# Attention and two expert layers on one core: another table for the order and the engine of each operation

## The chip, the core and the metric

The kernel runs on one core of a Trainium2 chip. A core has five engines with queues of their own: TensorE (PE: matrix products, from weights that it loads by PEld), VectorE (DVE), ScalarE (ACT), GpSimd (POOL) and SyncE (SP), which here only issues DMAs. Each engine runs its instructions strictly in the order in which the program gives them; between engines they wait on semaphores. The metric is the device time of one execution in microseconds.

## The reference

```
q_rot, k_rot = rotate(q), rotate(k)                 # 4 batches, 8 heads, 576 tokens, 64 wide
attn = softmax(q_rot @ k_rot.T / sqrt(64)) @ v      # max subtracted before exp
x = attn as 2304 tokens x 512
h = x @ w_in;  g = h * clip(h + 3, 0, 6) / 6;  x = g @ w_out       # layer 1, 512 -> 2048 -> 512
h = x @ w2_in; g = P(h) / (Q(h) + 1e-6);       out = g @ w2_out    # layer 2, same sizes
```

P is a cubic polynomial with coefficients a, and Q = 1 + |b0| |h| + |b1| h^2. All inputs and outputs are float32.

## The kernel before

Each float32 operand is split into a float16 high part and a float16 low part, and a product is made of three float16 products (high by high, high by low, low by high), summed in PSUM. So for each operand there is a cast to the high part, which ACT, DVE or POOL can do (the helper `copy`, whose instruction stands at L313 on ACT, L315 on POOL, L317 or L319 on DVE), and a subtraction that gives the low part.

*Attention* works in units of 128 queries for two heads (1152 score columns), and of 64 left-over queries (640 columns). PE writes the scores s into PSUM (L706 to L717), DVE reduces the maximum mx (L721), a small operation scales it (L724 to L729), ACT makes the exponentials e (L738). Then p is split: high part by `copy`, low part by the subtraction in L760, and a transposing DMA of SP (L763) writes both, turned, into pt, which PE multiplies with v (L796). A few early units use transposes on PE instead. The output xu is normalised (L814 to L826) and turned into xt for layer 1. Queries and keys come as nat, are turned by the rotary angles on DVE (L642, L649) and split.

*Layer 1* runs beside the attention of the following batch: matmuls h of 256 columns (L901), ACT's relu (L908), DVE's clip and product (L910) into t, high part gh by `copy`, low part gl by L914, and the second matmul (L929), which ACT or DVE evicts from PSUM (L935, shown as t<-h,d) and a DMA takes to y1d in DRAM.

*Layer 2* follows when all tokens have passed. It goes by blocks of 512 columns and pairs of feature tiles. A pair's 24 matmuls (L1148) fill a PSUM tile of 1024 columns, hh and hx in turn, one buffer each. The rational function reads it three times on ACT (lq L1157, ls L1158, lt L1159) and twice on DVE (L1163, L1164); after the last of these reads the tile is free for PE. DVE and ACT go on (L1161, L1166 to L1171) to lt, split into lgh (ACT, L1172) and lgl (DVE, L1173), and PE multiplies by w2o into ac (L1183), which goes to the output (ob). The last block has 256 columns. The layer's weights w2i and w2o are scaled and split at its start: the high parts by `copy` (L1050), the low parts by DVE (L1051).

What sets the order: the program makes 3527 operations as objects (`Plan.op`), and `Plan.order` decodes a table, `ORDER` (L93), into a list of pairs, operation and engine letter (P, A, D, G for PE, ACT, DVE, POOL; Q for SP's queue; N for none), with the PSUM bank of the operations that share two banks. The program issues the operations in this list's order, each on its engine, so that the table alone sets each queue.

```
code = np.cumsum(np.frombuffer(zlib.decompress(base64.b85decode("".join(ORDER))), "<u2"), ...) % 65536
for x in code:
    o, e = self.ops[x // 12], "PADGQN"[x % 12 // 2]
```

Of the kernel before, what the change touches and what calls it, by code (L numbers as in the profile page):

```python
# [23 lines left out]
H = 8  # L24
S = 576
D = 64
# [72 lines left out]
    'r)CMfqBr@In8|-Yqeecoz-<A{22c7`zqi`hr9q*<NHbPEwc!^+5=}>W5Y(U38s`S&3O;k1?=p7imT=#9@Q-8AF9h`q&vvxVJoglub9#;^HN0o<',
    'yX)zQ@J09!JerY1w_s5(fzq$1d~x4sbk6WCFddem+mjTTV6$ppAz#!AoAjgT1N7Y3l3y8rB7DPqXz!zPGVi(@4ZF7V>Xf|De%Q-Db`=`Ew8p<0',  # L100
    'tc5^yz%>+Ib1fP{dRJJW1!kvSD~vf)jSZL}wa#M5PpAxyf*9`i_E9lB=P8JG;9}>BUinr0#V*Z&A$?jXMJ{^>*Xt*qe0>0ca0t74fO+JWa2$KW',
    'je)KwIS*p1u@%%rMo}T$(pNpR#sG|KZxT#T;H_Ku3G~q=STK5Mie8zParM#*k!icZyAzs*wS?5GQC*>_LOa^f|19~xMP_92?Gb$;^ci<xpHA}Y',
    '=7H<JG<`K<^avF+1b1N<pTusP<HB87^vEE--GKW-no%me^l4|EbT|3nt;2alYdtepxrs%#3>7zj^3&h-j=en<yhaxk(+)TjE7kJk%!?sfo_s4D',
    'fD}hk49pXu#&{u!j@;NYbMD5lmLJ=I0yyUKVvmdlDL=NymnySDz-WdcF&B!}D)?8zpBhiZRP|KIb+oBxbcJH6BG$(T%{zuex~oo#%ixO58iiW-',
    'S1hs!%SxSa+tI4lNN>sarMB}bq0TW6YszD36<XYF=VekQw7M!ULhdd!Z=QJk7mUX;iHK4SdzVN}(C_S5rnwsWf5=bO;~O7E7va>XbnL5*Qorkt',
    'wyO%B3Oa723SK2we2qW0e_egerwWzulysxNGdQzSUZmM%HI`=*KGU&-(;_>3og>A<!laRBW{7^vAuJoEjzwGx2jOEm$w)C%6O*ki{X)1we&Bra',
    'E<;!ol1Q@puZ5ophjsv)dM=y_JGM*p$w}t1<G_5$cPN6C9?O6Xc~&=-Vd>bsE%X~}h9GsucIlYdt&WQSQ~iVv80Wqk{3<#V+oO++;u~wmpwR~D',
    '#<Wn+R4mQd^X;p;eD7jfNZ@~gFT89K>iGc5jBE*i#(&f7Fi28|@gL1ksp2lul8r4PAba2CIQOJ*B+W3Bn((WuO`6I^X^~_(Lpjm!eC1owzb8d8',
    '!tawoXDR;8*!Q$-xl=C@4(Wh;&#~n`wVU+e*qFFUQW&dujZb2qNDZKnTeJ%`7-js3dL%U%7V)7OAzi89bNNiXqBog}+)K-i5n&Zd@T<@gf6FNY',
    'M5@x^%?7Q6ZCaL|fAK0(Cd*8fM{o38RKb+pg*93MdvugcD|O=ZR}L?7VUuxsh14P~+$eP+6V;GK(#Sox??W%DB|d%DT@Qz$EYC6$(3#yHCGO+U',  # L110
    'fwvYqd=r=7(7xyDrIXl2A83c}A(D!l;8fWZ8|Wf*s~hw{8t|@!!pe^Go_-_}G7mfUkLcI*de<YIYHvrgq+eDqosY3-i^;3+mWUOtca=e3)N<A!',
    'AI-pfb_JAU0c~3AbUK;`-L3*W=?h=Higvr2qj#i5<vZ{RJ)+f8lDbE;q-xvG&C=IO)(1C(=b9kZ!nS>`)k|S=pgP>=TAkFPG=jsuhk^-z_}M2E',
    'yI*Vh?%e1e71`>$^oQ;-6t)`^r#>5(UV1i8o87}~Z%^sC`i9<@hLj8tQcpkIbWP)bQhq2+&>5u|*8OeaS!G$8qx;IbKk4%&Y0;k2mZeF$r<A$_',
    '=rvh@P47r(Nn7_9Up3Hmd<#EGD0){wLf&V=UL58fZvU0ymEp<f_x+VHsij&+q}#g?3i9{dfzKaEBMH@)KAxC${7v_SHXOPq`jN&}LvyG#;Zf*i',
    'LYc&czQ<y7Jzp8>6rZV~R0wT2mdz91PaB{*ROfqs`8;6^2F34&zRnA#z}WfB{Kzp9TTmLMJNz=8ylj+wd?oXg|3LmTnlM=$=TGeba>NFe_QV!i',
# [1174 lines left out]
```

## Time and profile before

| what | us |
|---|---|
| median of 3 runs | 1084.6 |
| fastest and slowest run | 1083.87, 1087.87 |
| the profiled execution | 1082.5 |
| its span (first to last instruction) | 1080.7 |
| PE busy in it | 982.2 |
| DVE, ACT, POOL busy | 905.7, 780.5, 61.2 |

Busy times of different engines lie beside each other and don't add up to the span. An engine's idle time matters only where what it waits for ends last. The span falls into the head (loads, splits of weights and the first units), attention beside layer 1, the end of layer 1, the entry of layer 2 and its body, and a tail. The clock in the rows is the share of full speed that was granted to PE: 1.00 is 2.4 GHz, and a mean of 0.86 over a stretch means that part of it ran at the lower level of 1.2 GHz.

### The profile page before, as it was taken

Reading aid. Unit: us, or ns where it says so; the run is one execution under the profiler, and the core shown is the slowest. Engines: PE = TensorE matmul, PEld = TensorE weight load, DVE = VectorE, ACT = ScalarE, POOL = GpSimd, SP = SyncE. Lnnn points to the kernel's source line nnn. Section 1 sums busy time; section 2 is a strip of 40 time slices with the busy share of each in tenths; the row PEclk is TensorE's granted clock in tenths of the full one; section 3 lists DMA queues with packets and bytes.
Section 4 is the critical chain, followed back from the end, with each engine's and each line's share of the span. In section 5 each row is a group of like instructions: output and inputs, shape, how many; then the busy total and the mean of one; then the engine's idle time right before and its main releaser. Section 6 shows DMA issues by size and latency. Waiting matters only on the chain.

```text
span 1080.7 us, 20026 instructions
## 1 busy us (share of the span) xinstructions
PE 982.2 (91%) x7973; PEld 695.0 (64%) x7978; DVE 905.7 (84%) x1408; ACT 780.5 (72%) x1219; POOL 61.2 (6%) x71
## 2 busy tenths in 40 slices
PE   1388799899999999999999989789999999999996
PEld 1277678788887888788888868234444444444563
DVE  5989998998999989888735695899799787977975
ACT  8989985877777766666738986685776766775763
POOL 0210010110111010120001010000000000000000
PEclk9998899999999999999999999889999999999998
DMA  8968677769889678587737742001011010010010
GB/s 279 265 160 239 120 125 145 170 122 175 145 171 186 139 135 144 102 155 140 133 65 259 229 170 70 10 0 39 1 40 40 1 39 1 20 39 1 1 40 19
DMA packets 253853, 117.04 MB, mean 108 GB/s; under 512 B 223552, under 2 KB 241088, under 8 KB 253760
## 3 DMA queue, kind: packets, MB, share of 16 engines
q1 hardware_dynamic: 253760, 115.77, 47.2%
q8 instruction: 62, 1.02, 0.4%
q14 instruction: 31, 0.25, 0.1%
HBM read 52.83 MB, written 9.44 MB: 58 GB/s over the span
## 4 chain that ended last, share of the span: by engine, by line
PE 63%; DVE 19%; ACT 9%; DMA 4%; issue 3%; POOL 1%; SPq 0%; ACTq 0%; DVEq 0%; POOLq 0%
PE ac L1183 13%; PE h L929 13%; PE h L901 10%; PE hh L1148 8%; PE hx L1148 7%; PE h L796 4%; PE s L706 3%; DVE mx L721 2%; DMA pt<-p 2%; DVE p L760 2%; DVE t L910 1%; DMA raw<-in_moe_w_in_dram 1%; PE h L787 1%; DVE lt L1163 1%; ACT e L738 1%
## 5 line engine op out<-in xcount | busy, mean ns | idle before, releaser
L901 PE MATMUL h<-xt,w 128*128 128x256 f16 x1728 | 199.7, 275 | 11.4 <-ACT xu L313 3.9
L901 PEld LDWEIGHTS <-w 128*128 128x128 f16 x1728 | 169.1, 99 | 33.6 <-issue 12.8
L929 PE MATMUL h<-gh,w 128*128 128x256 f16 x1080 | 190.3, 273 | 0.0
L929 PEld LDWEIGHTS <-w 128*128 128x128 f16 x1620 | 156.5, 98 | 18.8
L1183 PE MATMUL ac<-w2o,lgh 128*128 128x512 f16 x540 | 161.8, 382 | 3.3 <-ACT lgh L1172 3.3
L1148 PEld LDWEIGHTS <-w2i 128*128 128x128 f16 x900 | 89.1, 99 | 108.9 <-issue 24.0
L929 PE MATMUL h<-gl,w 128*128 128x256 f16 x540 | 147.2, 273 | 0.0
L738 ACT ACTIVATE e<-s,mx,qal 128x576 f32<-128x576 f32 (+1 forms) x144 | 114.5, 831 | 7.5 <-POOL mx L729 5.1
L1148 PE MATMUL hh<-x,w2i 128*128 128x512 f16 (+1 forms) x450 | 98.1, 365 | 8.5 <-ACT ls L1158 6.6
L1148 PE MATMUL hx<-x,w2i 128*128 128x512 f16 (+1 forms) x450 | 97.3, 364 | 6.7 <-ACT lq L1157 5.3
L1183 PE MATMUL ac<-w2o,lgl 128*128 128x512 f16 x270 | 102.8, 381 | 0.0
L721 DVE TENSOR_REDUCE mx<-s 128x2 f32<-128x1152 f32 (+1 forms) x80 | 99.1, 1242 | 3.7 <-PE s L709 3.2
L1183 PEld LDWEIGHTS <-lgh 128*128 128x128 f16 x576 | 56.5, 98 | 70.4 <-ACT lgh L1172 3.7
L760 DVE TENSOR_TENSOR p<-e,p 128x1152 f16<-128x1152 f32 (+1 forms) x72 | 89.2, 1239 | 11.3 <-ACT p L313 11.1
L1172 ACT ACTIVATE lgh<-lt 128x1024 f16<-128x1024 f32 (+1 forms) x40 | 38.6, 968 | 66.4 <-DVE lt L1171 43.8
L796 PE MATMUL h<-v,pt 128*128 128x130 f16 (+3 forms) x1440 | 77.4, 209 | 2.7 <-ACT xu L313 1.0
L908 ACT ACTIVATE t<-h,half,d 128x512 f32<-128x512 f32 (+1 forms) x96 | 61.6, 668 | 24.4 <-PE h L901 23.4
L796 PEld LDWEIGHTS <-pt 128*128 128x128 f16 (+1 forms) x1440 | 73.7, 102 | 7.3 <-issue 5.3
L313 ACT ACTIVATE p<-e 128x1152 f16<-128x1152 f32 (+1 forms) x61 | 64.3, 1054 | 12.1 <-DMA pt<-p 10.6
L706 PE MATMUL s<-qkt 64*128 64x512 f16 (+2 forms) x576 | 57.4, 326 | 8.8 <-ACT e L738 6.0
L1169 DVE SCALAR_TENSOR_TENSOR lt<-lt,cg,lr 128x1024 f32<-128x1024 f32 (+1 forms) x40 | 46.3, 1174 | 21.2 <-ACT lr L1167 21.2
L910 DVE SCALAR_TENSOR_TENSOR t<-t,h 128x512 f32<-128x512 f32 x72 | 48.9, 680 | 10.9 <-ACT t L908 10.4
(231 smaller groups left out, 1662.4 us busy)
## 6 DMA issues: line engine op xcount, KB each, us to landing
raw<-in_moe_w_in_dram SPq DMA_DIRECT2D x32, 512.0 KB, 5.1
raw<-in_moe_w_out_dram SPq DMA_DIRECT2D x32, 512.0 KB, 4.4
y1d<-t SPq DMA_DIRECT2D x18, 256.0 KB, 2.8
nat<-in_k_dram SPq DMA_DIRECT2D x16, 256.0 KB, 3.6
nat<-in_q_dram SPq DMA_DIRECT2D x16, 256.0 KB, 3.2
y<-y1d SPq DMA_DIRECT2D x16, 256.0 KB, 4.2
out_dram<-ob SPq DMA_DIRECT2D x16, 256.0 KB, 2.3
vnat<-in_v_dram SPq DMA_DIRECT2D x14, 256.0 KB, 2.9
```

Source lines behind the costliest of these rows:

```text
L313: act.activation(out, in_, AF.Copy, scale=scale)
L706: pe.matmul(s()[:, a:b], lhsT=kq(1, y, 64 * h, 64 * h + 64)[:, cc * 128:cc * 128 + 128], rhs=kq(0, z, 64 * h, 64 * h + 64)[:, c:c + b - a] ...
L721: op("D", c_dve(n), lambda e: vec.reduce_max(mx()[:, 0, 0:g], sv().rearrange("p (g n) -> p g n", g=g), axis=AX.X, negate=True), r=[s], w=[ ...
L738: act.activation(et()[:, h * (n // g):(h + 1) * (n // g)], sv()[:, h * (n // g):(h + 1) * (n // g)], AF.Exp, bias=mx()[:, 1, h:h + 1], sca ...
L760: op(EN("lo"), c_sub(n), lambda e: EL[e].tensor_tensor(ph()[:, n:2 * n], et()[:, 0:n], ph()[:, 0:n], ALU.subtract), r=es + [(ph, 0)], w=[( ...
L796: pe.matmul(ob()[r0:r0 + m, o:o + k], lhsT=w, rhs=vv[:, 0:k], start=(z == 0 and j == 0), stop=(z == 1 and j == 4))
L901: pe.matmul(hp()[:, o:o + NQ], lhsT=wt[kk]()[:, z, c:c + 128], rhs=x, start=(n == 0), stop=(n == 11))
L908: act.activation(seg(t, c, n), seg(hp, c, n), AF.Relu, bias=half(), scale=x()[:, g:g + 1])
L910: op("D", c_dve(2 * NQ), lambda e, t=t, hp=hp: vec.scalar_tensor_tensor(t(), t(), two(-15), hp()[:, 0:2 * NQ], ALU.min, ALU.mult), r=[hp], ...
L929: pe.matmul(yp()[:, o:o + NQ], lhsT=w[:, s_, m_ * 128:(m_ + 1) * 128], rhs=gt()[:, f], start=(f == 0 and z == 0), stop=(f == KF - 1 and z ...
L1148: pe.matmul(hp()[:, x * n:x * n + n], lhsT=wi[kk]()[:, z, c:c + 128], rhs=xt()[:, kk, y, 0:n], start=(i == 0), stop=(i == 11))
L1183: pe.matmul(accs[j][i]()[0:m], lhsT=gt()[:, y * n + x:y * n + x + m], rhs=wt, start=(f == 0 and z == 0), stop=(f == KF - 1 and z == 2))
```

## The change

Only the table is another. It has 64 lines in place of 67, so that every later line of the program has a number lower by 3.

```diff
@@ -91,73 +91,70 @@
 ORDER = (
-    'c-qx@flnMudgoWw(>*iYJ;Q)mc9!QQ1o2ox5FxV!5so015Dsw`=Ou_(gkuSdSmbjMOAvWM4rlo|uf=l2LWuY{mRKB%Sb_*a9A^>YI0SJ##34V9',
...
+    'c-l=_4@?~Cb${Rd+hJyQSz|)?Hk?BUb&-o4WD$bgjfE(6C`B%^h>Iw4iG>hy=><9NX>&p@@*$UV2tqD(s6|{vsYP6JMJ}?aODQ=aN-fUfEJ7TM',
...
 )
```

The 3527 operations and what they compute are the same. On PE the same 7859 instructions follow in nearly the same order (neighbours are swapped; the farthest move is 9 places). DVE has 1376 instructions in place of 1408, ACT 1053 activations in place of 1105, POOL 151 in place of 67. SP gives 20 DMA issues to ACT: 3 of raw weights, 6 of y1, 2 of y1d, 6 of queries, 3 of values.

Operations that change their engine, over the whole program: from DVE to POOL 16 subtractions L760 (13 of 1152 columns, 3 of 640), 18 subtractions L914 (12 of them between 210 and 560 us of the trace of before, 6 after), 13 operations of the rotary stage, 3 casts of p, 4 of xu, 3 maxima, 2 of gh, 3 casts of layer-2 weights. From ACT to POOL 8 casts gh, 8 maxima, 6 casts of p, 5 in the rotary stage, 10 casts of weights, and two others. From ACT to DVE 11 maxima, 6 casts of p, 8 evictions of xu, 3 casts gh, 6 of weights, and four others. From DVE to ACT 4 casts of p, 3 evictions of layer 1 and 2 maxima. From POOL to ACT 4 of v and 2 maxima, to DVE 3 each of gh, maxima and xu.

Three places follow. The first is ACT's queue where layer 1 ends and layer 2 begins (h_75 and h_76 are the two PSUM banks of layer 1, w2qs a scale, x_9240 the split input of a later block). Before:

```order
L313 ACTIVATE t<-h_75,d 128x2x64 x4
L313 ACTIVATE w2i_9170<-w2o_8364,w2qs 128x512
L313 ACTIVATE w2o_9185<-w2o_8407,w2qs 128x512
L313 ACTIVATE w2o_9200<-w2o_8484,w2qs 128x512
L313 ACTIVATE w2o_9209<-w2o_8466,w2qs 128x512
L313 ACTIVATE w2o_9212<-w2o_8521,w2qs 128x512
L1159 ACTIVATE lt<-hh,cg 128x1024
L1069 ACTIVATE x_9240<-y_8781 128x512 x4
L1157 ACTIVATE lq<-hh,cf 128x1024
L313 ACTIVATE w2o_9250<-w2o_8591,w2qs 128x512
L1158 ACTIVATE ls<-hh,dv 128x1024
```

After:

```order
L310 ACTIVATE t<-h_75,d 128x2x64 x4
L441 ACTIVATE junk,w2am<-w2o_8953 128x512
L310 ACTIVATE t<-h_76,d 128x2x64 x4
L938 DMA y1d<-t 128x2x256
L1156 ACTIVATE lt<-hh,cg 128x1024
L1155 ACTIVATE ls<-hh,dv 128x1024
L310 ACTIVATE w2o_9256<-w2o_8596,w2qs 128x512
L1154 ACTIVATE lq<-hh,cf 128x1024
```

Before, five casts of weights (one of w2i, four of w2o) stand between the eviction t and the first read of hh, and four casts of x and one of w2o among its reads. After, both evictions are ACT's, no cast stands ahead of the first read, and one stands among the reads.

The second is ACT's queue in the last block of layer 2, which has 512 columns in each tile. Before:

```order
L1159 ACTIVATE lt<-hh,cg 128x512
L1159 ACTIVATE lt<-hx,cg 128x512
L1157 ACTIVATE lq<-hh,cf 128x512
L1157 ACTIVATE lq<-hx,cf 128x512
L1158 ACTIVATE ls<-hh,dv 128x512
L1158 ACTIVATE ls<-hx,dv 128x512
L1166 ACTIVATE lr<-lq,qb 128x512 x2
L1167 ACTIVATE lr<-lr 128x512 x2
L1172 ACTIVATE lgh<-lt 128x512 x2
```

After:

```order
L1156 ACTIVATE lt<-hh,cg 128x512
L1169 ACTIVATE lgh<-lt 128x512
L1155 ACTIVATE ls<-hh,dv 128x512
L1169 ACTIVATE lgh<-lt 128x512
L1154 ACTIVATE lq<-hh,cf 128x512
L1156 ACTIVATE lt<-hx,cg 128x512
L1154 ACTIVATE lq<-hx,cf 128x512
L1155 ACTIVATE ls<-hx,dv 128x512
L1163 ACTIVATE lr<-lq,qb 128x512
L1164 ACTIVATE lr<-lr 128x512
```

Before, each step of hx follows the same step of hh. After, the reads of hh stand first, among them the last step (lgh) of the pair ahead, and those of hx behind them.

The third is POOL's queue in the middle of attention, beside layer 1 (the numbers behind p, xu and v are buffers). Before:

```order
L315 TENSOR_SCALAR xu_714<-xu_714 128x256
L315 TENSOR_SCALAR gh<-t 128x512 x3
L315 TENSOR_SCALAR v_111<-vnat_97,qps 128x10x64
L729 TENSOR_SCALAR mx<-mx,qal 128x2
L315 TENSOR_SCALAR xu_714<-xu_714 128x256
```

After:

```order
L757 TENSOR_TENSOR p_2980<-e,p_2980 128x1152
L312 TENSOR_SCALAR xu_742<-xu_742 128x256
L757 TENSOR_TENSOR p_3154<-e,p_3154 128x1152
L757 TENSOR_TENSOR p_3157<-e,p_3157 128x1152
L312 TENSOR_SCALAR xu_592<-xu_592 128x256
L312 TENSOR_SCALAR p_3301<-e 128x1152
L911 TENSOR_TENSOR gl<-t,gh 128x512
```

Before, POOL has only operations with one input tile. After, subtractions of two tiles, p and gl, stand among its casts.

## Rows read from the trace of the kernel before

**Rows 1.** the page: busy time, share of the span and instructions of each engine

```profile
PE 982.2 (91%) x7973; PEld 695.0 (64%) x7978; DVE 905.7 (84%) x1408; ACT 780.5 (72%) x1219; POOL 61.2 (6%) x71
```

**Rows 2.** windows: length; PE, PEld, DVE, ACT, POOL busy; clock; DMA; GB/s

```profile
0.00:150.00 150.00, 93.98 (x707) 80.31 (x708) 133.06 (x267) 135.22 (x282) 12.72 (x17) 0.95 0.79 206
150.00:560.00 410.00, 399.18 (x4516) 343.12 (x4515) 362.60 (x580) 285.85 (x457) 39.22 (x45) 1.00 0.76 141
560.00:676.00 116.00, 109.74 (x941) 92.69 (x941) 73.77 (x152) 90.68 (x181) 9.24 (x9) 0.99 0.54 178
676.00:726.00 50.00, 37.32 (x146) 15.42 (x147) 43.34 (x47) 37.65 (x42) 0.00 (x0) 0.86 0.02 6
726.00:1040.00 314.00, 310.51 (x1492) 145.92 (x1493) 270.88 (x333) 210.53 (x227) 0.00 (x0) 1.00 0.06 19
```

**Rows 3.** timeline of PE, 686 to 726 us: start, duration, instruction, [idle before <-releaser]

```profile
686.40 8.16 PE L1148 MATMUL hh<-x,w2i 128*128 128x512 f16 x24 [4.65 <-ACT ls L1158]
...
702.20 5.34 PE L1148 MATMUL hh<-x,w2i 128*128 128x512 f16 x24 [1.85 <-ACT lq L1157]
...
718.07 7.70 PE L1148 MATMUL hx<-x,w2i 128*128 128x512 f16 x24 [5.35 <-ACT lq L1157]
```

**Rows 4.** timeline of ACT and DVE, 673 to 685 us

```profile
673.38 0.72 ACT L313 ACTIVATE w2o<-w2o,w2qs 128x512 f16<-128x512 f32 x1 [0.82 <-DVE w2i L1051]
674.14 0.75 DVE L1051 SCALAR_TENSOR_TENSOR w2o<-w2o,w2qs,w2o 128x512 f16<-128x512 f32 x1 [0.79 <-ACT w2o L313]
675.22 1.13 DVE L319 TENSOR_SCALAR t<-h,d 128x128 f32<-128x128 f32 x4 [0.33 <-PE h L929]
...
679.21 1.19 ACT L1159 ACTIVATE lt<-hh,cg 128x1024 f32<-128x1024 f32 x1
...
682.32 1.27 DVE L1164 SCALAR_TENSOR_TENSOR lt<-lt,cg,hh 128x1024 f32<-128x1024 f32 x1
683.62 1.11 ACT L1157 ACTIVATE lq<-hh,cf 128x1024 f32<-128x1024 f32 x1 [1.15 <-DVE lt L1164]
```

**Rows 5.** chain that ended last, from 1050 us: start, duration, piece

```profile
1054.15 2.63 PE hh L1148 x24
...
1067.80 6.95 PE ac L1183 x24
```

**Rows 6.** waits: who <- releaser: us in all, number, longest

```profile
PE ac L1183 <- ACT lgh L1172: 3.3, 1, 3.3
PE h L901 <- DVE t L910: 3.3, 3, 2.5
```

**Rows 7.** groups by line and shape: xcount | busy us, mean ns | idle before

```profile
L760 DVE TENSOR_TENSOR p<-e,p 128x1152 f16<-128x1152 f32 x56 | 75.7, 1351 | 9.6 <-ACT p L313 9.5
L914 DVE TENSOR_TENSOR gl<-t,gh 128x512 f16<-128x512 f32 x72 | 49.2, 684 | 6.2 <-ACT gh L313 3.0 <-POOL gh L315 3.0
L319 DVE TENSOR_SCALAR w2i<-w2i,w2ps 128x512 f16<-128x512 f32 x10 | 4.8, 483 | 0.1
L908 ACT ACTIVATE t<-h,half,d 128x128 f32<-128x128 f32 x32 | 12.0, 456 | 3.2 <-PE h L901 2.7 <-DVE gu L1101 0.4
```

**Rows 8.** timelines of POOL and DVE around 140 and 231 us

```profile
140.75 0.62 POOL L315 TENSOR_SCALAR gh<-t 128x512 f16<-128x512 f32 x1 [3.53 <-DVE t L910]
140.64 1.36 DVE L721 TENSOR_REDUCE mx<-s 128x2 f32<-128x1152 f32 x1
...
230.69 1.48 DVE L649 TENSOR_TENSOR nat<-nat,tab 128x1280 f32<-128x1280 f32 x1
230.84 1.80 POOL L315 TENSOR_SCALAR gh<-t 128x512 f16<-128x512 f32 x1 [11.75 <-DVE t L910]
232.68 0.69 DVE L914 TENSOR_TENSOR gl<-t,gh 128x512 f16<-128x512 f32 x1 [0.52 <-POOL gh L315]
```

**Rows 9.** SP's queue: an issue in the timeline, and waits of the transposing DMA

```profile
18.11 0.53 SPq L412 DMA_DIRECT2D raw<-in_moe_w_in_dram  x1
...
SPq L763 <- DVE p L760: 31.8, 18, 4.4
```

More of the change, by code (lines that the diff above doesn't have):

```diff
@@ L99 @@
[L99 to L103, printed above, removed]
@@ new lines @@
+    'fh8!l^Xak@b*5NITou|-T9^sWc^H=K@SKZQG1*{u<<WGz&;^sq11P2?utWlI)moHe1e}Nxfjf-*rqJGiPTGPRm~tyo?fd>9w8H5AdEXj6O+KQ(',
+    'ug3N_r46^wi$b|ljwfF6ne499BTu6@Hf)n^`*AP31Xf~)4k}R?vr81y?o-Cm8xgoF*CoOMll?>DT_p&8%DF@!P-f3rGtkafpwlneH_?7c2p5E4',
+    '>*En9m19mhwEDa7=_7kX?y&<9S6bm~>?1n@FW5sii_z>Y$p18|biue?YVS&Jx=U>I$8yI$9>SC6ab2sTCTe|+zg7F`T0z^#At>_);O1U$FbLI%',
+    'gEi=2M%u`+tTq@`3Sf#U_7I#AXT(x_+S+2mo5R~}h`}b9qrGIUK>M`Lo6Ir5*zXQpurGNdqyv4qjuC7}`={7i!M%@z>Qw&F>q#~YA$h<WRa;r3',
+    ')b2+1*XVTa2|K3z3HvK@&)Slo!F`zbM_JSBFnpN*FZ<(&fl-tcv`;CWL<0(=u&S?q;u_U@)9Y0^l)JDsrA}v>Xar8PtG+ullsmD18_%snuh%QX',
@@ new lines @@
+    '_B48opIfcWTaAcF12v2I>%o9)iT3zU1Ft1F)9W97?cgaB)+p}UVxR<IQ!2~6lvFt3R{2+6H)E{aFKn?++Qw$~H~nLYCMb}cOaW#>cZz4B$-3D^',
+    'qk{c==7)AMN*~nJ)W%oi>y|WQHppk>+RU=FV8)bAX%?o<evHzXeio*jMrqP%m+!$tb4nkg`I&aPBWHw22cw7~lbtn#5XoPCU2FWp+e=mG2E-jH',
+    ';J!9MQWWR1F~T;I<?uMCN1r_~%-_|1o8%FTR&O^4!)VVj5>K4a0x+7>V3&Ad0rNBYT#Lf6V@qEq0rQ1cmfDb`%5!g-1VJ?m)djCndYOtF;pAx}',
+    '03Rd+@S&_jqtCJoc*Fu|vj!#NW2;!Ym1%MUFeT^tF!FGeenn{~H>?W5vOZ86?B{lw-+)|OhdFyk3nAiTPN_TsSHVe+=~3srG4YuO0cBGXlw*6l',
+    '+FKbezX@N<QmI;)bd9GwXOvaDOS!HL*bj_vCv{|y09>$_gAY=}cG1yA`-7~XKbF2_-aOj3({8lVUD<X11N`u=qr(U*(u&-;cxEpE53=#R=yQ_+',
@@ new lines @@
+    'qs+X`>I`eA=;(E;HB$xe$$qGIt^~H&#{OUAeCeRtMwBUF1V2-c29XIPN-r6pPnboIxtlbk<Yxwz0oo__yRV!L<pDC|AdNYVzIW13eG9Pa^^%Ds',
+    '_sBOu$GjRzv`NEiE1g58zQpdMKMQiZys2cn!Pg+a;j0O1y^)jw=9lt7i_NP|cyA>y`npu8VMAW8&?*eO<)#6}vY@W#ZSL%1cI6{Z&m9CI>Rj^&',
+    '@OhP4;V-2zan#$$E84A0<Uy5xMCd?Nj<NcKliFQ~dHE!tRHRDvSLRnyx9yy1l+l}7_JzfmIjq((SL`-ZzFc_I(vkh@pk6gd6a=gwv+kDg+?!$x',
+    '>Err1TcuAAHs7GXY|ELT=i#(ac%(L7ZAR4~jHC@H(>GiVR?^MtHrq|VVD)-4`{xvo-V);H9evTQ5GK8Nx*YG!`yyzIhPxhU+#BcFK(KLlhpJXF',
+    'X#SX^l2BUEIe)rlp`J1SMvt0pIb*_xGb5^G+TXi(Hoc_QrK{cu$GcfDU8tWzKfYi+xM$Q1hEK;EXzP)g-Rnon_kV8cFv0k#clAbpG#-TEgJ{m=',
@@ new lines @@
+    'e+Koa5YBj`hYV;wP#ty*95x|ooR!=>D3j(gt<rszvhFqDw6TSjl;Z?)$y-40mSf%-pQFABvz_-G+_nPIWDk*l0?39ntW@|F4zCf+D#|Uqi}!jM',
+    'pTj%p4D<-~DD@%KW*Hc~0CeN3>k`i(NR_JPzroWuB~tz##nZZ3AxnV7rm`K-G(M>%D_%A2l#ZjPZe|u>L%f6$4a1PfF(#oO@>o%}d!KQqgpfFs',
+    '*(7VE64~S?k&xB+(>0op--pplr^GN^^>}m)I0c+-YLM^nRE%7ocM_+T6ZnnuL^0()ETD~~g{-oh=p}yL&8ob&#6Eb!V+>*OFoGjc;WmivxaI<D',
+    'B@gH^jC6_k(47>Y;nOLXTUjJr$M5UdyB&uheTXw-H+z7Sb2sC^AXMUK6n5xY!hdIPXXgm_TQv*f=W*a%I-NzL>(&U@(AL|+6ua>`MjYh7HssPR',
+    '#@BLGU0{cG4>`&?hO;2gQ5UtS5pY^^5QRzz=DfrDvVc(vKpk5+jHf-MT(`#+CyNS`{U4sA1Jn',
```

104 lines of the change are left out of this document (43 added, 61 removed).

## The prediction

> **What bounds the kernel now.** I read the page's busy shares first. TensorE (PE) is busy 982.2 us, 91% of the span of 1080.7 [rows 1]; VectorE (DVE) has 84%, ScalarE (ACT) 72%, GpSimd (POOL) 6%. The order can therefore win back at most the 98.5 us in which PE is idle, and what PE loses where its clock had dropped. Next I read the windows by stage, to see where those 98.5 us lie [rows 2]. Of the head (0 to 150 us) PE misses 56 us, and there DVE (133.06) and ACT (135.22) are nearly full: the head is theirs. From 150 to 560 us, attention beside layer 1, PE misses 10.8 of 410 us and DVE is busy 362.6, so 47 us of DVE are spare. The end of layer 1 (560 to 676) misses 6.3 us, the entry of layer 2 (676 to 726) 12.7 us at a mean clock of 0.86, the body of layer 2 (726 to 1040) 3.5 us with DVE at 270.88 of 314, and what is left to the end of the span about 9 us. DVE's 84% is thus a mean over a full head, a full entry (43.34 of 50) and stages with room. In the middle and in the body of layer 2 a lighter DVE is worth little.
>
> Last I read the two places outside the head with long stops. At the entry of layer 2, PE waits 4.65, 1.85 and 5.35 us for the rational function to read its PSUM banks [rows 3]. The 24 matmuls behind the first stop take 8.16 us and those behind the third 7.70, where the 24 behind the short second one take 5.34: two stops leave PE at a lower granted clock. Together 4.65 + 1.85 + 5.35 + 2.82 + 2.36 = 17.0 us. ACT and DVE at that place show why [rows 4]: five 0.72 us weight casts stand on ACT one behind the other, each with a DVE subtraction of 0.75 behind it, and the layer-1 eviction (1.13) stands between them on DVE; the rational function's first DVE steps end at 683.6, and only then does ACT read the bank again. At the tail, hx and hh of the last block are done at 1056.8 and the first output matmul behind them starts at 1067.80; its 24 take 6.95 us in place of 5.34 [rows 5]. Of those 11 us PE stands still for 3.3 [rows 6]; work of the block before fills the rest. Place and price: 3.3 + 1.6 = 4.9 us.
>
> **The change, part by part.** Nothing is added to or taken from the arithmetic. PE's order moves only by swaps of neighbours. The table hands work from DVE and ACT to POOL, whose instructions go from 67 to 151 (engine calls in the program), moves 20 DMA issues from SP's queue to ACT's, and reorders DVE and ACT.
>
> *Entry of layer 2.* The last layer-1 matmul ends at 675.2 [rows 4]. In the new order ACT does the second half of the eviction too (4 x 0.456 = 1.8, by the row for ACT's reads of 128 columns [rows 7]) and is at 677.0; PE's hx then starts 0.6 us later than now. Of the casts ahead of the rational function, seven leave ACT and only one stands between its first reads. ACT: lt to 678.2 (1.19), ls to 679.3, one cast to 680.0, lq to 681.2 (1.11 each). DVE runs from 671.8: five casts and six subtractions at (0.48 + 0.75) x 5 + 0.75 = 6.9 gives 678.7, by [rows 4, 7], with the casts that POOL takes ready in time; then its two steps on hh, 1.27 at most each, to 681.2. hx's 24 matmuls end at 677.0 + 5.34 = 682.3. By then hh has been read, so PE need not stop, and hh ends at 687.7 where the trace has 694.6: a lead of 7 us. It can't be kept whole: DVE has only 6.66 us of idle time in this stretch [rows 2] and gets three casts, +1.4. But the clock losses (5.2) go with the stops, and the later stage has 43 us of DVE to make good. I take -8; bounds -3 (only the first stop goes, most of the lead is lost again) and -13 (17.0 less about 4 us of stops).
>
> *Tail.* Now hh and hx go through the rational function in pairs, so that the first output waits for both. In the new order hh runs ahead, and its output matmuls cover hx's chain. Of 4.9 us I take -4; bounds 0 (the chain of hh alone is still longer than what PE has left) and -5.
>
> *End of layer 1.* Three waits of 3.3 us in all for DVE's t [rows 6], of PE's 6.3 us idle. The evictions go to ACT, six gl subtractions and some casts to POOL. ACT is the fuller engine there (90.68 of 116) and gains the evictions: -1.5; bounds -4 and 0.
>
> *Head.* DVE loses about 8 us of work and ACT about 5 (rope steps, maxima and casts to POOL, which has 12.72 of 150 busy [rows 2]). If these two set the head, 5 us is the most. But the head's first steps form one chain, in which a slower POOL step counts in full: -1.5; bounds -5 and +6.
>
> *The middle, 150 to 560.* DVE gives POOL 12 wide p subtractions (the low half of the exponentials), 3 narrower ones and 12 gl subtractions: 12 x 1.351 + 3 x 0.75 (by their share of the columns) + 12 x 0.684 = 27 us [rows 7]. PE can gain no more than 10.8 here, and DVE was not what it waited for. The unknown is POOL's price. No row of before shows POOL subtracting one tile from another; the nearest are its casts with one input. One of 512 columns takes 0.62 us beside a DVE maximum read from PSUM, and 1.80 beside DVE's L649, which works on two SBUF tiles [rows 8]. By the lower rate, 1.21 ns a column, the 27 cost POOL 12 x 1.40 + 3 x 0.78 + 12 x 0.62 = 26.5 us, hardly more than they cost DVE; by the upper, 3.5 ns, 12 x 4.05 + 3 x 2.25 + 12 x 1.80 = 77 us. POOL has 370 us free, so its time costs nothing by itself. If DVE is held through all of POOL's time, it needs 47 + 24 = 71 us of it (spare time plus what net leaves it) before DVE becomes the bound: only the upper end would do that, and then by 6 us. So 0, with bounds -5 and +22 (first rival). I lean to the lower half because in the new order the instruction next to a moved subtraction on DVE is in about 9 of 16 cases the maximum from PSUM, the neighbour of the 0.62 row.
>
> The Trainium skill has a rule that speaks against this (SBUF — State Buffer, section "SBUF: two separate sides"): DVE and GpSimd share a port pair as an exclusive lock, and a DVE operation with two SBUF inputs and a GpSimd one that reads SBUF shut each other out for a whole instruction. The trace agrees: that 1.80 us cast started 0.15 us after L649 and ended 0.47 us behind it, and DVE's gl waited 0.52 for it [rows 8]. The skill also has a price (GPSIMD Engine Reference, section "Elementwise — side-by-side cycle accounting"): 1.96 times DVE for an operation on two tensors; by it the 27 subtractions would hold the pair for an estimated 53 us, under the 71, and the sum would stay.
>
> *DMA issues on ACT.* SP takes 0.53 us to issue a raw load [rows 9]. Twenty on ACT are at most 10.6 us, spread over stages where ACT has room; two fall in the head and about four around the entry, so up to 4 us if each holds a read that PE waits for. SP's gain is small: 18 of its transposing pt issues wait for DVE's p, 31.8 us in all [rows 9], but they run ahead of PE. I take 0.
>
> *Sum.* -8 - 4 - 1.5 - 1.5 + 0 = -15 on the profiled execution's 1082.5 us, about 1067.5 to 1069. The median of the runs is 2.1 higher than that execution, so as a median about 1070.6; I say 1071. By their bounds the terms give -27 to +19 if all fell the same way; half of that on the good side is 1060.
>
> **The rivals.** *First, slower: POOL's subtractions arrive late.* A p subtraction stands between exp and the transposing DMA that PE's value matmuls need. At 4.05 us in place of 1.35 each of the 16 in the whole program comes 2.7 us later, 43 us in all; if half of that shows, PE loses 22 us in the middle: 1084.6 - 14 + 22 = 1093. It decides from 1.2 us of PE time per moved p subtraction ((14 + 5.4)/16). For it: a POOL step can be three times as slow [rows 8], and DVE stands still meanwhile. Against it: the PE queue has other work there (layer 1 beside attention), and DVE's p sets 18 pt issues already without PE stopping for it, in a stage with 10.8 us of PE idle time. The skill's lock rule is this rival's mechanism. Chance 0.14.
>
> *Second, the same: the entry's lead is lost to DVE's backlog.* DVE is full from 676 to 726 [rows 2] and gets 1.4 us more. If it only moves the stop from ACT to DVE, the entry yields 2 and the tail 2, the rest nothing: about 1081. For it: the third stop, 5.35, is one DVE made by being late for ACT. Against it: the clock. Chance 0.16.
>
> *Third: all stops close.* Entry -13, tail -5, end of layer 1 -3, head -4: 1060. Chance 0.12. *Fourth: DMA issues hold ACT,* +4 on the forecast, 1075: inside my forecast's range.
>
> **How the numbers follow.** My forecast (1064 to 1079, 1071 likeliest) has 0.58. About 0.5%, 5.4 us, is what a measurement of this kernel can tell from no change, so faster is under 1079.2 and slower over 1090. Faster: 0.58 + 0.12 = 0.70; same 0.16; slower 0.14. The range 1060 to 1090 leaves out most of the first rival and the far side of the third.
>
> **What would show it.** Right: in the stretch behind the last layer-1 matmul no PE stop over 2 us and 24 matmuls in about 5.3; the last block's output matmuls at 5.3 for 24 and a wait under 1 us ahead of them; POOL's wide subtractions between 1.4 and 4.05 us, with DVE's idle time in 150 to 560 under 71 us and PE's under 12 there. Wrong: PE waiting in 150 to 560 for pt transfers whose releaser is POOL (first rival); a stop of 5 us at the entry with DVE as its releaser (second); a head longer than 150 us at the same point of the program.

## The result

The changed kernel is slower: 1099.41 us median (1099.17 to 1100.45), against 1084.24 for the kernel before in the same comparison. The ratio is 1.0113, 95% interval 1.0085 to 1.0140, so about 12 us where 13.6 us less were forecast; the time lies above the range that was given. The profiled execution of the changed kernel has a span of 1097.4 us, 16.7 more than that of before.

The head of the page and the windows by stage, of the changed kernel, answer to [rows 1, 2]. The windows are cut at nearly the same places of the program as there (columns as in [rows 2]):

```profile
span 1097.4 us, 20037 instructions
...
PE 983.6 (90%) x7978; PEld 693.3 (63%) x7978; DVE 908.7 (83%) x1376; ACT 749.3 (68%) x1167; POOL 178.8 (16%) x155
```

```profile
0.00:160.00 160.00, 95.21 (x707) 80.41 (x708) 131.91 (x254) 132.68 (x273) 37.39 (x36) 0.88 0.72 191
160.00:579.00 419.00, 399.39 (x4511) 341.61 (x4509) 369.39 (x573) 266.94 (x422) 110.42 (x90) 1.00 0.76 138
579.00:691.00 112.00, 108.88 (x950) 92.67 (x948) 70.83 (x138) 86.38 (x177) 26.19 (x26) 1.00 0.56 184
691.00:741.00 50.00, 40.96 (x165) 17.20 (x165) 42.63 (x47) 34.21 (x38) 4.79 (x4) 0.90 0.02 6
741.00:1062.00 321.00, 309.06 (x1472) 143.88 (x1471) 270.61 (x332) 209.06 (x229) 0.00 (x0) 0.99 0.06 19
```

DVE has 32 instructions fewer than before and is busy 3 us longer; in the middle (second row) it is busy 369 us, though it gave away 27. The head is 10 us longer at a lower clock, the middle 9 longer, the end of layer 1 4 shorter, and the body of layer 2 (last row), where POOL does nothing in either kernel, 7 longer with 20 matmuls fewer in it.

To compare kernels stage by stage I took from each trace the time at which PE had ended the same number of matmuls (8.5%, 79% and all of layer 1's 3456; 26% of layer 2's 1824, just ahead of its first change of block, and 98%; the end of the span; in the trace of before 176, 580, 675, 793, 1062 and 1081 us) and from that how much longer than before each piece is, in us:

```
                      head  middle  end of   entry     body     tail    span
                                    layer 1  (layer 2) (layer 2)
changed kernel       +11.7    +7.0   -3.8     -4.4    +11.9    -5.7   +16.7
e1_subs_back          +7.1    +1.0   -3.3     -4.9    +13.7    -5.7    +7.9
g4_p_back            +11.9     0.0   -3.5     -4.4    +11.9    -5.7   +10.2
e2_pool_back          +9.1    +6.3   -2.3     -1.2    +12.0    -5.7   +18.1
h2_issue_sp          +10.7    +5.1   -2.3     -3.3    +11.3    -5.7   +15.8
e7_head_before        +3.9    +5.6   -3.8     -3.3    +12.0    -5.7    +8.6
f1_order_only        +15.2   +15.5   -2.5     +0.3    +11.1    -5.7   +33.9
f2_engines_only       +6.8   +16.2   +0.5     -2.2      0.0    -0.1   +21.1
e3_subs_pool          +7.3    -0.2   -1.8     -0.1      0.0    -0.1    +5.2
e4_layer2_after       +1.7    +0.1    0.0     -5.2    +12.5    -5.7    +3.4
f3_entry_tail         +7.1    +0.1   +0.6     +3.5      0.0    -5.7    +5.5
g3_head_after        +12.4    +1.6   +0.1     +0.5      0.0    +0.2   +14.8
h1_head_pool_back    +10.8    +4.1   -1.2     +0.1      0.0    +0.1   +14.0
g1_end_entry_tail     +1.7    -2.0   -3.8     +2.4      0.0    -5.7    -7.4
g2_tail               +0.2    +0.7   -0.5     -0.2      0.0    -5.7    -5.5
h3_end_tail           +0.9    +0.3   -3.8     +0.2      0.0    -5.7    -8.1
```

Where a kernel has the code of before, its head reads up to 7 us longer, its middle between 2 shorter and 2 longer (once, in h1, 4 longer), and its last pieces repeat within 1.2 us, where no seam between the two tables lies in them: so much one execution differs from another. With the changed order the cut between head and middle is not sharp: at 16% of layer 1's matmuls in place of 8.5% up to 4 us would go from the head to the middle. Single executions of the kernel before lay between 1078 and 1091 us, so the verdicts below are ratios over many runs of both kernels on one chip.

### The profile page after: what moved, and what is told of

Its sections match the earlier page's. It is cut to its first block, busy times and chain, and to the rows that moved or that the text cites. A ratio compares the mean times of both kernels' runs of the same rounds, so it can differ in the third digit from the quotient of the medians.

```text
span 1097.4 us, 20037 instructions
## 1 busy us (share of the span) xinstructions
PE 983.6 (90%) x7978; PEld 693.3 (63%) x7978; DVE 908.7 (83%) x1376; ACT 749.3 (68%) x1167; POOL 178.8 (16%) x155
## 5 line engine op out<-in xcount | busy, mean ns | idle before, releaser
L898 PE MATMUL h<-xt,w 128*128 128x256 f16 x1728 | 196.8, 272 | 7.8 <-ACT xu L310 3.6
L1145 PEld LDWEIGHTS <-w2i 128*128 128x128 f16 x900 | 89.3, 100 | 107.4 <-issue 16.2
L793 PEld LDWEIGHTS <-pt 128*128 128x128 f16 (+1 forms) x1440 | 72.6, 101 | 15.1 <-issue 12.5
L757 DVE TENSOR_TENSOR p<-e,p 128x1152 f16<-128x1152 f32 (+1 forms) x56 | 69.8, 1246 | 11.3 <-ACT p L310 11.2
L310 ACT ACTIVATE p<-e 128x1152 f16<-128x1152 f32 (+1 forms) x53 | 57.1, 1080 | 14.4 <-DMA pt<-p 13.9
L1163 ACT ACTIVATE lr<-lq,qb 128x1024 f32<-128x1024 f32 (+1 forms) x40 | 42.3, 1059 | 33.9 <-DVE lq L1158 33.9
L703 PEld LDWEIGHTS <-qkt 64*128 64x128 f16 x576 | 35.6, 99 | 40.4 <-issue 27.5
L907 DVE SCALAR_TENSOR_TENSOR t<-t,h 128x512 f32<-128x512 f32 x72 | 48.9, 681 | 14.0 <-ACT t L905 13.6
```

Of the source, the lines that this page charges most:

```text
L310: act.activation(out, in_, AF.Copy, scale=scale)
L703: pe.matmul(s()[:, a:b], lhsT=kq(1, y, 64 * h, 64 * h + 64)[:, cc * 128:cc * 128 + 128], rhs=kq(0, z, 64 * h, 64 * h + 64)[:, c:c + b - a] ...
L757: op(EN("lo"), c_sub(n), lambda e: EL[e].tensor_tensor(ph()[:, n:2 * n], et()[:, 0:n], ph()[:, 0:n], ALU.subtract), r=es + [(ph, 0)], w=[( ...
L793: pe.matmul(ob()[r0:r0 + m, o:o + k], lhsT=w, rhs=vv[:, 0:k], start=(z == 0 and j == 0), stop=(z == 1 and j == 4))
L898: pe.matmul(hp()[:, o:o + NQ], lhsT=wt[kk]()[:, z, c:c + 128], rhs=x, start=(n == 0), stop=(n == 11))
L1145: pe.matmul(hp()[:, x * n:x * n + n], lhsT=wi[kk]()[:, z, c:c + 128], rhs=xt()[:, kk, y, 0:n], start=(i == 0), stop=(i == 11))
```

## The experiments

The program is the same in all of them; only the table is another, so the edits are given as pairs of operation and engine, in the order of one table or the other. D, A, G and Q are DVE, ACT, POOL and SP's queue; lines are those of before.

**e1: the subtractions back on DVE.**

```diff
 # changed table, same order
-(p L760, G) x16   (gl L914, G) x18
+(p L760, D) x16   (gl L914, D) x18
```

> The changed table, with only the 34 subtractions (16 of p, 18 of gl) given back from GpSimd to VectorE, each at its place in the order. Theory A (GpSimd's subtractions hold VectorE and come late): the changed kernel loses about 8 us against before in the middle (150 to 580 us of its trace); these 34 are 62 of GpSimd's 179 us there, so most of the 8 goes, about 1091. Theory B (the order itself, or something else than GpSimd, costs the time): VectorE gets 32 us of work back, nothing else gets better, 1099 or more.

Measured: 1.0066 of before (1.0046 to 1.0085), 5 us better than the changed kernel's 1.0113. The middle's extra falls from 7.0 to 1.0, which is within what kernels with the old middle show. In the body nothing is won. The head of this one trace reads 4.6 us less than the changed kernel's; g4 below, with the same head, reads as much as the changed kernel.

**e2: all of POOL's new work back.**

```diff
 # changed table, same order
-(62 operations of DVE and 40 of ACT, G)
+(the same, engine of before)
```

> The changed table, with all 102 operations that it newly puts on GpSimd given back to the engine that had them before (62 to VectorE, 40 to ScalarE), order unchanged. Theory A, widened to all of GpSimd's work: the 10 us lost in the head go too, together about 1081. Theory B: the head and the middle stay as long as they are, 1099 or longer, since VectorE and ScalarE get some 60 us of work.

Measured: 1.0130 (1.0103 to 1.0156), no better than the changed kernel. The middle is 6.3 us longer again, the body 12.0, and the entry 1.2 shorter instead of 4.4. What the 34 subtractions win back in e1 is lost when all 102 operations go back: in this order DVE and ACT need the work taken from them, and theory A in its wide form fell.

**e3: the same subtractions on POOL, in the old table.**

```diff
 # table of before, same order
-(p L760, D) x16   (gl L914, D) x18
+(p L760, G) x16   (gl L914, G) x18
```

> The table of before, with only those same 34 subtractions on GpSimd, at their old places. Theory A: slower by about what e1 gains, 1090 to 1095, with VectorE's other rows longer than before. Theory B: VectorE is 32 us lighter and had nothing to wait for, 1080 to 1085.

Measured: 0.9982 (0.9962 to 1.0002). The moved subtractions cost nothing that shows in the order of before. So what they cost in the changed kernel is not their duration as such but depends on what stands beside and behind them.

**e4: layer 2 of the changed table on the layer 1 of before.**

```diff
-operations 2545 to 3527 of the table of before
+those left, in the order and on the engines of the changed table
```

> The order and engines of before up to the last matmuls of layer 1, those of the changed table from there (entry, body and tail of layer 2). Read from the two traces, the changed table gains some 3 us at the entry and 5 at the tail, and loses some 9 us in the body, where GpSimd does nothing. If the order in the body is the cause: 1084 to 1087, with TensorE's stops at the changes of block as in the changed kernel. If the body's loss was carried in from the late layer 1: it goes, 1076.

Measured: 1.0005 (0.9983 to 1.0026). Entry -5.2, body +12.5, tail -5.7, as in the changed kernel, behind a layer 1 that is not late. The body's loss is its own. Three of PE's stops in the body of e4, from the timeline of PE: one for the eviction of the finished block, and two for steps on DVE that find the scale of the next block's input:

```profile
794.12 1.01 PE L1183 MATMUL ac<-w2i,lgh 128*128 128x512 f16 x2 [2.91 <-ACT ob L313]
...
859.38 0.39 PE L1183 MATMUL ac<-w2o,lgl 128*128 128x512 f16 x1 [2.22 <-DVE gi L1103]
...
995.56 4.69 PE L1148 MATMUL hh<-x,w2i 128*128 128x512 f16 x21 [2.00 <-DVE y1m L1081]
```

**f1, f2: the order without the engines, the engines without the order.**

```diff
 # f1: changed table's order, engine of before for every operation
 # f2: order of before, changed table's engine for every operation
```

> The changed order, but every operation on the engine that it had before. After the runs above: moving the 34 subtractions to GpSimd cost nothing in the old order, and giving them back in the new one won 5 us. Theory C (the order costs time by itself, in the head and in the body of layer 2, and the moved work costs in the middle alone): head and body lost as in the changed kernel, middle as before: 1.005 to 1.010 of before. Theory D (the engines of the new table are what costs, the order only in the body): head and middle as before, body 7 us late, entry and tail gained, 1.000.

> The order of before, with every operation on the engine that the changed table gives it. Theory C: the middle loses what it lost in the changed kernel or less, head and body nothing, 1.000 to 1.006. Theory D: 1.012 or more, since the order of before was made for other engines.

Measured: f1 1.0283 (1.0227 to 1.0338), f2 1.0153 (1.0114 to 1.0192). The order alone is worse than both together, and the engines alone are no better (f2's interval overlaps the changed kernel's); in the middle they cost 15.5 and 16.2 us. Order and engines go together, and neither theory had that. f2 also says that the engines cost nothing in the body (0.0) and f1 that the order does (+11.1).

**f3: only entry and tail of the changed table.**

```diff
 # table of before, but
-operations 2545 to 2690 and 3410 to 3527 in the order of before
+those in the order and on the engines of the changed table
```

> The table of before, with the changed table's order and engines at the entry of layer 2 (its last layer-1 matmuls to the first rational functions) and at the tail alone; the body of layer 2 as before. If entry and tail are worth what the profile of e4 shows (stops and clock at the entry 17.0 against 11.7 us, tail 5): 8 to 10 us, 0.991. If the body of before gives the entry's gain back, as the time that it had to spare: 5 us, 0.9955. It would beat both kernels in either case.

Measured: 0.9979 (0.9952 to 1.0007). The entry's lead was taken back at the seam: the body of before soon asks for a small matmul into hh, and PE stood still for it.

```profile
739.37 0.61 PE L1079 MATMUL hh<-x,ones 128*128 128x512 bf16 x1 [6.59 <-DVE lt L1164]
```

PE had a lead at this place and DVE, which it waits for, had none. It is the second rival of the prediction in small: with DVE full there, what PE wins at the entry must be spent on work that doesn't wait for DVE.

**e7, g3, h1: the head.**

```diff
 # e7: the first 590 operations from the table of before, the rest from the changed one
 # g3: the first 590 from the changed table, the rest from that of before
 # h1: as g3, but
-(15 operations of DVE and 4 of ACT in the head, G)
+(the same, engine of before)
```

> The changed table with the first 590 operations (the head, to about 150 us) in the order and on the engines of before. If the head's own table costs the 6 to 10 us that the traces show there: 1.003 of before, 8 us under the changed kernel. If the head's difference is what one execution differs from another (heads of equal code lay up to 7 us apart above): 1.010, hardly less than the changed kernel.

> The changed table's first 590 operations (the head), and all others as before. e7 puts the price of this head at 7 us, 1.0065. If that is only TensorE's lower clock at 100 to 120 us (0.50 in the traces of the changed kernel, but also in those of e3 and f3, whose head is that of before), runs of this kernel and of before fall on the same two times, and the ratio is under 1.003.

> As g3 (the changed table's first 590 operations, the rest as before), but with the 19 operations that it newly puts on GpSimd there given back to VectorE (15) and ScalarE (4), at the same places. If the head's 5 to 7 us are GpSimd's slower rotary steps at its start (the first rot took 2.04 us there, 0.85 on VectorE) and its holding of VectorE: 1.000. If it is the head's order: 1.005 as g3, or more.

Measured: e7 1.0047 (1.0022 to 1.0072), g3 1.0050 (1.0026 to 1.0074), h1 1.0094 (1.0071 to 1.0116). By e7 and g3 the new head costs 5 to 7 us. If it were PE's lower clock alone, g3 was to be under 1.003; 1.0050 speaks against that, though the interval reaches down to 1.0026. g3's fastest and slowest runs, 1086.33 and 1097.29 us, also lie 7 to 8 us above those of before on its chip (1078.15 and 1090.49). Giving POOL's work back makes the head no shorter: the order, with the engines of before, is enough for the loss, and my theory of the slow rotary steps fell. That POOL has no part in it isn't shown, since in f2 the old order with the new engines has a longer head as well (+6.8). The stretch from 100 to 120 us, of before, the changed kernel, h1 and f3 (columns as in [rows 2]), shows one thing that goes with the order, though not with it alone:

```profile
100.00:120.00 20.00, 15.50 (x143) 13.29 (x142) 19.99 (x37) 19.89 (x45) 0.97 (x1) 0.93 0.61 171
```

```profile
100.00:120.00 20.00, 18.16 (x91) 16.08 (x91) 14.41 (x26) 15.47 (x33) 5.28 (x5) 0.50 0.47 154
```

```profile
100.00:120.00 20.00, 18.88 (x95) 16.31 (x97) 15.27 (x30) 17.41 (x39) 0.00 (x0) 0.50 0.53 174
```

```profile
100.00:120.00 20.00, 19.02 (x116) 16.36 (x114) 15.15 (x28) 15.29 (x34) 0.97 (x1) 0.58 0.51 150
```

In the changed kernel PE runs the whole stretch at a granted clock of 0.50 (1.2 GHz) and issues 91 matmuls where before issued 143. h1, with the same order, too. But f3, whose head is word for word that of before, fell to 0.58 as well, and e3, whose head differs from it by one p subtraction on POOL, to 0.57, while e4, g2 and h3 with the head of before stayed at 0.91 or above. The old head falls in some executions, and the new order did in all of its traces (0.50 to 0.52) but e1's (0.80), where the clock was low before 100 us instead (0.59 between 60 and 80 us, against 0.97 in the changed kernel). Some 2 to 4 us of the new head are there before this stretch: the first transposes of the exponentials (L753) start at 56.56 us in the changed kernel, at 55.90 in h1 and at 54.82 in g3, against 52.72 before. How much of the 5 to 7 us is the clock and how much this late start can't be told from these runs.

**g4: only the p subtractions back.**

```diff
 # changed table, same order
-(p L760, G) x16
+(p L760, D) x16
```

> The changed table with only the 16 p subtractions given back to VectorE; the 18 gl subtractions stay on GpSimd. If the lateness of p (2.43 in place of 1.35 us ahead of the transposing DMA) is what the middle loses: as e1, 1.0066 of before. If it is GpSimd's holding of VectorE, which the gl subtractions (25 us of GpSimd) do as well: about half of e1's gain, 1.009.

Measured: 1.0054 (1.0024 to 1.0083), as e1, with the 18 gl subtractions still on POOL. The middle reads 0.0 in place of +7.0. Of the 34 subtractions the 16 of p are the cost. Whether by coming late or by holding DVE, this run alone doesn't tell, since the excess of DVE's rows falls with them too, to about half (see the middle, below).

**g1, g2, h3: what the changed table does well, alone.**

```diff
 # table of before, with these operations in the order and on the engines of the changed one:
 # g1: 2150 to 2830 and 3410 to 3527   (end of layer 1, entry to the first change of block, tail)
 # g2: 3410 to 3527                    (tail)
 # h3: 2150 to 2545 and 3410 to 3527   (end of layer 1, tail)
```

> The table of before, with the changed table from operation 2150 (the last batch's layer 1 alone) to 2830 (just ahead of the first change of block in layer 2) and again from 3410 (the tail). By the traces of the changed kernel and of e4: end of layer 1 -3.5, entry -5.5 (kept to the end of the first block), tail -5; the body's changes of block as before. If each keeps what it showed there: 0.987 of before. If the lead is taken back at the seam, as in f3, where TensorE stopped 6.6 us for VectorE: only end and tail, 0.992.

> The table of before with the changed table's last 117 operations alone (the tail, from 3410). If running hh's chain ahead of hx's is what the tail gained in the changed kernel (5 us by its trace) and nothing before it is needed for it: 0.9955. If the gain there rests on the later body (work of the block before lying there as cover): 1.000.

> The table of before with the changed table's end of layer 1 (operations 2150 to 2545) and tail (from 3410). By the traces of g1 and g2: -4 and -6, 0.990. If g1's whole gain over before came from its tail and its end of layer 1 brought nothing: 0.9925, as g2.

Measured: g1 0.9914 (0.9889 to 0.9940), g2 0.9925 (0.9901 to 0.9949), h3 0.9913 (0.9886 to 0.9941). The tail is a gain by itself. By the traces the end of layer 1 adds 3 to 4 us to it, which the intervals of g2 and h3 can't show. g1's entry lead was lost at its seam, which lies at the cut of the table above, and adds nothing. All three beat both kernels; h3's median is 1076.64 us, 10.6 under the 1087.28 that before took on its chip.

**h2: the DMA issues back on SP.**

```diff
 # changed table, same order
-(20 DMA issues: raw, q, v, y1, y1d, A)
+(20 DMA issues: raw, q, v, y1, y1d, Q)
```

> The changed kernel with its 20 DMA issues on ScalarE's queue given back to SP's. If they hold ScalarE's reads (the fourth rival of the prediction): up to 4 us better than the changed kernel, 1.0075 of before, and the stops at the changes of block shorter, since 4 of the moved operations load the next block there. If not: 1.011.

Measured: 1.0086 (1.0053 to 1.0119): the interval reaches from a gain of 6 us on the changed kernel's 1.0113 to none. The body is about as long as without the edit (+11.3 against +11.9), so the issues are not its cause. Whether they cost a microsecond or two in the head stays open.

## Why the prediction was wrong, term by term

**The entry (-8 forecast, -4.4 measured)** came within its bounds, at about half, and not as worked out. The stops of PE there, answering to [rows 3]:

```profile
700.33 6.85 PE L1145 MATMUL hh<-x,w2i 128*128 128x512 f16 x24 [3.65 <-ACT lq L1154]
709.85 7.04 PE L1145 MATMUL hx<-x,w2i 128*128 128x512 f16 x24 [2.67 <-DVE lt L1161]
719.27 7.04 PE L1145 MATMUL hh<-x,w2i 128*128 128x512 f16 x24 [2.39 <-DVE lt L1161]
```

Stops and slow matmuls now make 8.7 + 4.9 = 13.6 us where they made 17.0. I had worked out that PE need not stop at all. The step that failed is that ACT would read hh three times one behind the other. ACT and DVE of the changed kernel at that place ([rows 4] of before):

```profile
691.74 1.20 ACT L1156 ACTIVATE lt<-hh,cg 128x1024 f32<-128x1024 f32 x1 [0.46 <-DVE w2o L316]
697.55 1.11 ACT L1155 ACTIVATE ls<-hh,dv 128x1024 f32<-128x1024 f32 x1 [4.61 <-DVE lt L1161]
...
699.17 1.10 ACT L1154 ACTIVATE lq<-hh,cf 128x1024 f32<-128x1024 f32 x1
```

```profile
694.99 1.21 DVE L1160 TENSOR_TENSOR lt<-lt,hh 128x1024 f32<-128x1024 f32 x1
696.24 1.28 DVE L1161 SCALAR_TENSOR_TENSOR lt<-lt,cg,hh 128x1024 f32<-128x1024 f32 x1
```

On ACT's queue ls stands right behind lt, and yet it starts 0.03 us after the end of DVE's last read of hh, of whose result it uses nothing. In the table ls comes behind that read. Where ACT and DVE read one PSUM tile, the built program kept the table's order between them as well, and that can't be seen in the order of either engine alone. In none of the traces of this case does a read of hh or hx by ACT overlap one of the same tile by DVE. The row of before had shown it, too: lq at 683.62 waits 1.15 us for DVE's lt [rows 4], and I took it for a matter of ACT's being late. DVE, for its part, went from its weight casts to the two steps at 694.99, 4.9 us after the last layer-1 matmul; I had 3.5, with the casts of POOL ready in time, and for one of them DVE waited 0.82 us.

**The body of layer 2 (not in the sum, +11.9 measured)** is the largest error: the sum has no term for it. I had read PE's 3.5 us of idle time there as a bound on what could be won and said nothing of what could be lost, because the engines' work is the same. Only the order matters: e4 (+12.5) shows the loss without a late layer 1, f1 (+11.1) with the engines of before, f2 (0.0) that the engines alone bring none of it, h2 that the DMA issues have no part. The waits of PE in the body are 11.9 us in all against 3.3, which is most of the loss. The longest of the changed kernel (741 to 1062 us), then all of before (726 to 1040):

```profile
PE ac L1180 <- ACT ob L310: 3.6, 2, 2.9
PE hh L1076 <- DVE lt L1161: 3.1, 2, 1.6
PE ac L1180 <- DVE gi L1100: 2.2, 1, 2.2
PE hh L1145 <- DVE y1m L1078: 2.0, 1, 2.0
```

```profile
PE hh L1148 <- ACT ls L1158: 2.4, 3, 1.0
PE hx L1148 <- ACT ls L1158: 0.9, 1, 0.9
```

At the first change of block of the changed kernel, on ACT and PE:

```profile
801.92 1.11 ACT L1154 ACTIVATE lq<-hh,cf 128x1024 f32<-128x1024 f32 x1 [2.07 <-DVE lt L1160]
...
804.40 0.68 ACT L310 ACTIVATE ob<-ac,cg 128x512 f32<-128x512 f32 x1
...
805.49 0.69 ACT L310 ACTIVATE ob<-ac,cg 128x512 f32<-128x512 f32 x1
...
807.23 0.69 ACT L310 ACTIVATE ob<-ac,cg 128x512 f32<-128x512 f32 x1
...
809.85 0.69 ACT L310 ACTIVATE ob<-ac,cg 128x512 f32<-128x512 f32 x1
```

```profile
807.97 0.59 PE L1180 MATMUL ac<-w2i,lgh 128*128 128x512 f16 x2 [2.91 <-ACT ob L310]
```

The four evictions of the finished block stand behind a read of hh that waits 2.07 us for DVE, and squares of the next block and steps of the rational function stand between them; PE's next block needs the banks and waits 2.91 us. Before, the same four evictions go in two pairs, from 795.23 and 799.19 us, and PE has no stop there:

```profile
795.23 1.27 ACT L313 ACTIVATE ob<-ac,cg 128x512 f32<-128x512 f32 x2
...
799.19 1.25 ACT L313 ACTIVATE ob<-ac,cg 128x512 f32<-128x512 f32 x2
```

Two more stops, of some 2 us each, are among the rows of e4 above. These rows show which waits end last; which of the moved steps must go back was not tried.

**The middle (0 forecast, bounds -5 to +22; +7.0 measured)** lay inside its bounds and was wrong in its value. PE is idle there for 19.6 us in place of 10.8 (419.00 - 399.39 in the second window); I had set under 12 as a sign of being right. The price of POOL's subtraction lay in the range, and steady. Groups by line and shape, of the changed kernel:

```profile
L757 POOL TENSOR_TENSOR p<-e,p 128x1152 f16<-128x1152 f32 x13 | 31.6, 2432 | 30.2 <-ACT p L310 15.7 <-DVE p L314 8.5 <-issue 5.7
...
L911 POOL TENSOR_TENSOR gl<-t,gh 128x512 f16<-128x512 f32 x18 | 25.2, 1398 | 38.2 <-ACT gh L310 17.3 <-DVE d L886 8.8 <-DVE gh L314 4.8
```

2.43 us, between my 1.40 and 4.05. The Trainium skill's 1.96 times DVE (GPSIMD Engine Reference, section "Elementwise — side-by-side cycle accounting") is for 2048 columns and gives an estimate of 2.65; 2.43 is 1.80 times DVE's 1.351 [rows 7]. What these instructions do to DVE is seen in two of them, on POOL and DVE of the changed kernel:

```profile
259.48 2.37 POOL L757 TENSOR_TENSOR p<-e,p 128x1152 f16<-128x1152 f32 x1 [1.81 <-DVE p L314]
...
271.38 2.37 POOL L757 TENSOR_TENSOR p<-e,p 128x1152 f16<-128x1152 f32 x1 [1.77 <-issue]
```

```profile
259.72 2.42 DVE L811 TENSOR_TENSOR xu<-xu 128x256 f32<-128x256 f32 x1
...
271.54 1.36 DVE L718 TENSOR_REDUCE mx<-s 128x2 f32<-128x1152 f32 x1
```

Beside the first, DVE's addition of two SBUF tiles, 0.42 us before, takes 2.42 and ends 0.29 us behind POOL; beside the second, the maximum from PSUM takes its usual 1.36. This is the exclusive lock of the Trainium skill (SBUF — State Buffer, section "SBUF: two separate sides"), and the rows agree with it. In the whole trace of the changed kernel 27 DVE instructions that read PSUM lie beside one of the 34 subtractions, and none is longer than the quick price of its shape by more than 0.01 us; of 20 that work on two SBUF tiles, 11 are longer by 0.36 to 2.19 us. I had leaned on PSUM neighbours in 9 of 16 cases; the others can pay nearly the whole of POOL's time. Over the middle DVE's rows are some 35 us longer than the same shapes at their quick price, against 6 before and 17 in g4 (each row's excess over the lower quartile of its shape in the trace of before; all of POOL's work counts in it, not the subtractions alone). The 27 us that DVE was to save are gone, as the 369.39 in the second window shows. DVE is still not the bound, as I said; but its steps come late, and PE's value matmuls, which need a PSUM bank that DVE's t frees, wait for it. From the waits of PE in the middle, changed kernel and g4:

```profile
PE h L793 <- DVE t L907: 7.5, 7, 1.8
```

```profile
PE h L796 <- DVE t L910: 3.7, 4, 1.8
```

In the trace of before this wait is 0.7 us in all, so that it makes 6.8 of the 8.8 us by which PE is longer idle. So the first rival happened, at about a third of the 22 us that I gave it, and by these waits mostly not by its path: SP's pt issues wait for POOL's p three times only (the waits of SP's queue, answering to [rows 9]).

```profile
SPq L760 <- POOL p L757: 4.7, 3, 2.6
```

e3 adds that all 34 cost nothing that shows in the old order, where DVE's rows are only some 18 us over their quick prices and PE's wait for t is 1.0 us.

**The head (-1.5 forecast, 5 to 7 measured by e7 and g3)** lay near the upper bound of +6. The bound's reason, a slower POOL step in the first chain, isn't needed for the loss (h1): the new order brings it with the old engines too. By what path it does so stays open; a lower clock of PE and a later start go with it.

**End of layer 1 (-1.5; -3.8) and tail (-4; -5.7)** went the way that was forecast and were a little small. Of the three waits that I had put into the end of layer 1 [rows 6], two, of 2.8 us, lie in it. For the tail the mechanism is seen. The chain that ended last in the changed kernel has in it

```profile
1079.14 12.32 PE ac L1180 x57
```

57 output matmuls without a stop at full pace (0.216 us each), where before stopped for 3.3 us and then took 6.95 us for 24 [rows 5, 6], at a granted clock of 0.79 between 1067 and 1075 us. It carries over unharmed by itself (g2), and the end of layer 1 with it (h3).

**DMA issues on ACT (0):** h2 gives no ground to change that.

In sum: terms of -8 - 1.5 - 4 became -4.4 - 3.8 - 5.7. That their total is nearly the forecast one is luck, as the entry gave half and the other two more. What failed were the three zeros and near zeros: head, middle and body gave 11.7 + 7.0 + 11.9 by the traces (the head's by an execution at the low clock; 5 to 7 by the runs). The bounds, too, were added up wrongly: as given they make -32 and +25, not -27 and +19, and they have no term for the body. I had costed moved work by engine and asked of each stage only whether its bounding engine got lighter. I didn't ask what a stage in which PE hardly waits can lose by another order.

## What to carry to other kernels

A table of orders is a gain or a loss stage by stage, and its stages can be taken apart: keep the pieces that win (here tail and end of layer 1, together 0.991) and drop the rest. Where PE has almost no idle time, a reordering has little to win and much to lose (here 3.5 us against 11.9); look there for steps that stand ahead of an eviction that frees PSUM. In these traces a two-tile instruction moved to POOL could cost DVE nearly its whole duration where DVE's neighbour works on two SBUF tiles, and cost nothing where the neighbour reads PSUM.

## What the runs showed of the hardware

PE's granted clock between 100 and 120 us falls to 0.58 in one execution (f3) and stays at 0.91 to 0.93 in others of word for word the same head (before, e4, g2, h3; g1 and e7 lie between, at 0.67 and 0.63). In the table of pieces f3's head reads +7.1 and those of the others at the high clock 0.2 to 1.7: 5 us and more of 1084, as much as several of the edits that were to be judged. That the clock is the cause of the longer head isn't shown; g1's reads only +1.7. POOL's subtraction of 1152 columns took the same 2.37 us with DVE held beside it and with DVE running; DVE's 0.42 us instruction took 2.42. And two readers of one PSUM tile on different engines kept the table's order.
